# First loads as f32 by two other queues, f32 transposes, x in halves, and one written order, in a one-core attention and gated feed-forward kernel

## The chip, the core and the metric

The kernel runs on one core of a Trainium2 chip. The metric is the device time of one execution in microseconds, lower is better. A core has TensorE (PE, matmuls; its weight loads are listed as PEld), VectorE (DVE), ScalarE (ACT), GpSimd (POOL) and SyncE (SP). POOL, SP and ACT can issue DMAs, each from its own queue and in its own order; a DMA that changes the type of the data on the way is issued by POOL in this kernel.

## The reference, cut to what matters

```python
# attention: 4 batches, 8 heads, 768 positions, 64 per head, all f32
scores = q @ k.transpose(0, 1, 3, 2) / 8
# heads 0, 2, 6: causal; heads 1, 3, 4, 5, 7: the last 64 positions, and positions 0 to 3
a = softmax(where(mask, scores, -1e9))
x = (a @ v).transpose(0, 2, 1, 3).reshape(3072, 512)
# gated feed-forward on 3072 tokens
g = x @ w_gate                      # 512 x 1536
h = gelu(g) * (x @ w_val)           # 512 x 1536
ffn = h @ w_out                     # 1536 x 512
out = x + sigmoid(x @ w_res) * ffn  # 512 x 512
```

## The kernel before

The 3072 tokens are cut into six chunks of four 128-row tiles (`CHUNKS`; chunks 1 and 4 span two batches). For each chunk the kernel does attention for four pairs of heads (`PAIRS`: 0 = heads 0, 2; 1 = 4, 6; 2 = 1, 3; 3 = 5, 7), turns the result to features by tokens (`xT`), makes gate and value (`gate_value`; the blocks of the last six of twelve feature rows by a scheme with seven products for eight, `fast`, with copies `seed` and `hold` and sums `merge` between its matmuls), and then the output (`output`, `output_fast`, also with seven products: copies `keep`, sums `plus`).

Queries and keys are loaded by POOL, which makes f16 of them on the way, into `qks` (L678); for the first two chunks PE turns them (L824, `qkT`) and ACT or DVE evacuates (L835, `qkE`), later ones are turned by DMA (L868). Scores are L1012 (row tiling: two half-height matmuls side by side) and L1103 (first four keys, quarter tiling), exponentials L1028, L1032, L1110, masks L1064, weighted values L616 and L1136 (column tiling). A reciprocal (L1190) and a multiply (L1203, `norm`) give f32 `xtok`, and for chunk 0 and the odd heads a second multiply (L1201, `norm16`) gives f16 `x16`, which PE turns (L1225, evacuated by L1233, `xE`). `xtok` has two buffers of a whole chunk, [128, 4, 512] f32. Chunks 1 to 4 store x to the output (L1443, `store_x`), and the rest is added to it by DMA (L1522); chunks 0 and 5 add x on DVE or POOL (L1528, L1568) and store the sum (L1534, L1572).

Every operation is recorded as a task with the tasks that it needs and the buffers that it uses. `schedule` lays them out: a list per engine (`PLAN`, five lists of task numbers, and a sixth with buffer places) is followed by a model of the time, which also puts dummy matmuls (L1578, `warm`) where PE would stand. Each engine then runs its list in order and waits on semaphores. A PE task has a tiling (`mode`); tasks with `able` may also run in column tiling (matmuls of L617: two half-width ones), which is kept where the task before left it so:

```python
stay = tiling == t.mode or tiling in t.able
if not stay:
    tiling = next(iter(t.able), t.mode)
```

PSUM has eight banks. Each kind of use has its banks and a cap; the products of `fast` run in the three pairs that the first three gate and value blocks of the chunk used (`LANES`).

Of the kernel before, what the change touches and what calls it, by code (L numbers as in the profile page):

```python
# [4 lines left out]
NHEAD = 8  # L5
# [42 lines left out]
LANES = 3  # L48


HINTS = (
)

PLAN = (
# [83 lines left out]
class Task:  # L138
# [4 lines left out]
    def __init__(self, eng, dur, fn, deps, prio, bufs=(), fset=None, dma=0.0, order=(), name="", grp=None):  # L143
# [4 lines left out]
        self.users = []  # L148
        self.ready = 0.0
        self.end = None  # L150
        self.done = None
        self.signal = False
        self.name = name
        self.sem = None
# [24 lines left out]


class Pool:
    def __init__(self, items, caps=None):
        self.items = items
        self.caps = caps or {}
        self.held = {}
# [1494 lines left out]
```

## Time and profile before

| | |
|---|---|
| median of 3 runs (lowest, highest) | 264.08 us (262.93, 264.22) |
| profiled execution, span from first to last instruction | 261.9 us |
| TensorE clock granted, mean | 0.998 |
| PE, DVE, ACT, POOL busy | 253.3, 202.2, 169.0, 107.7 us |
| DMA packets, of these under 512 B | 102068, 88720 |
| HBM read, written | 29.36 MB, 10.49 MB |

The profile gives the span of the profiled execution; its own whole time isn't listed apart from the three runs, which lie 1.0 to 2.3 us above the span. Times in rows are microseconds from the start of the span. A group's row gives line, engine, operation, output<-inputs and shapes, then busy time, mean ns of one, and the idle time ahead with what ended it. PE matmuls are pipelined: the time between starts is the time that one takes up, and the listed duration is longer.

### The profile page before, as it was taken

The page shows a single profiled execution, that of the slowest core. Times are in us where ns is not written, and L with a number is a line of the kernel's source. Part 1 is how long each engine was busy: PE and PEld are TensorE (multiplying, and loading weights), DVE is VectorE, ACT ScalarE, POOL GpSimd, SP SyncE. Part 2 cuts the span into 40 slices and gives each one's busy share as a digit, 9 for nine tenths or more (in the row PEclk, how much of TensorE's full clock was granted, in tenths as well). Part 3 has the DMA queues.
Part 4 walks back from the last instruction along what each step waited for, and adds up shares of the span by engine and source line. Part 5 has one row for each costly group of instructions (what it writes and reads, how often), then busy time and mean ns, then how long its engine had stood idle before and what let it go on. Part 6 is the DMA issues. An engine that isn't in the chain of part 4 may idle for free.

```text
span 261.9 us, 8109 instructions
## 1 busy us (share of the span) xinstructions
PE 253.3 (97%) x3436; PEld 181.4 (69%) x3436; DVE 202.2 (77%) x443; ACT 169.0 (65%) x303; POOL 107.7 (41%) x146
## 2 busy tenths in 40 slices
PE   7899999999999999999999999999999998999992
PEld 5568655458577477667578577689687677788891
DVE  2587449788888987868988788978687986678974
ACT  2488537795676997467896566896465994564511
POOL 8899918970061964243998330001110040010032
PEclk9999999999999999999999999999999999999999
DMA  7999999999989999999999999607940029060003
GB/s 67 162 186 191 196 191 194 183 170 153 168 226 136 154 138 143 209 178 129 128 93 110 151 199 130 204 5 116 228 104 1 3 22 137 12 80 4 3 22 141
DMA packets 102068, 33.18 MB, mean 127 GB/s; under 512 B 88720, under 2 KB 97168, under 8 KB 102032
## 3 DMA queue, kind: packets, MB, share of 16 engines
q0 software_dynamic: 74704, 18.88, 82.4%
q1 hardware_dynamic: 27040, 13.52, 26.0%
q8 instruction: 27, 0.44, 0.8%
q10 hardware_dynamic: 288, 0.26, 0.3%
q14 instruction: 9, 0.07, 0.1%
HBM read 29.36 MB, written 10.49 MB: 152 GB/s over the span
## 4 chain that ended last, share of the span: by engine, by line
PE 93%; DMA 2%; DVE 1%; issue 1%; POOL 1%; DVEq 0%; POOLq 0%
PE ps L616 47%; PE ps L617 33%; PE ps L1012 6%; DMA qks<-in_q_dram 2%; PE ps L1136 2%; PE ps L1578 2%; PE ps L1225 2%; PE ps L824 1%; PE ps L1103 1%; POOL qks L678 1%; DVE otile L1518 0%; DVE otile L1528 0%; DVE xtok L1203 0%; DVE ea L1064 0%; DVE rcp L1190 0%
## 5 line engine op out<-in xcount | busy, mean ns | idle before, releaser
L1522 POOL DMA_DIRECT2D out_dram<-otile x16 | 14.9, 966 | 87.9 <-DVE otile L1518 65.8
L678 POOL DMA_DIRECT2D qks<-in_k_dram x37 | 31.4, 892 | 31.7 <-DMA kT<-qks 24.3
L616 PE MATMUL ps<-xT,wg 128*128 128x512 f16 (+1 forms) x172 | 38.7, 337 | 0.0
L1291 ACT ACTIVATE gact<-ps 128x512 f16<-128x512 f32 x38 | 21.9, 596 | 22.9 <-PE ps L616 14.8
L1293 DVE SCALAR_TENSOR_TENSOR hT<-gact,ps 128x512 f16<-128x512 f16 x38 | 25.9, 686 | 12.5 <-PE ps L616 6.7
L616 PE MATMUL ps<-xT,wv 128*128 128x512 f16 (+1 forms) x160 | 35.3, 334 | 0.0
L678 POOL DMA_DIRECT2D qks<-in_q_dram x37 | 31.0, 867 | 6.8 <-PE ps L824 6.8
L1365 DVE TENSOR_TENSOR ps<-ps,otile 128x256 f32<-128x256 f32 x60 | 25.0, 430 | 6.3 <-PE ps L617 2.6
L678 POOL DMA_DIRECT2D va<-in_v_dram x24 | 24.3, 1021 | 0.0
L1028 ACT ACTIVATE ea<-ps 128x1024 f16<-128x1024 f32 (+2 forms) x24 | 21.5, 917 | 3.9 <-PE ps L1012 3.7
L1383 ACT ACTIVATE gact<-ps 128x512 f16<-128x512 f32 x30 | 16.5, 594 | 10.4 <-PE ps L616 6.0
L616 PEld LDWEIGHTS ps<-xT,wg 128*128 128x128 f16 x172 | 16.6, 98 | 9.5 <-DVE hT L1293 0.4
L616 PEld LDWEIGHTS ps<-xT,wv 128*128 128x128 f16 x160 | 15.3, 98 | 10.6 <-issue 0.4
L1390 DVE SCALAR_TENSOR_TENSOR hT<-gact,ps 128x512 f16<-128x512 f16 x30 | 19.5, 682 | 3.3 <-PE ps L616 1.8
L617 PE MATMUL ps<-xT,wv 128*64 128x512 f16 (+1 forms) x168 | 20.8, 350 | 0.0
L616 PE MATMUL ps<-wo,hT 128*128 128x256 f16 (+1 forms) x114 | 18.8, 296 | 0.0
L1494 DVE TENSOR_TENSOR otile<-otile,ps 128x256 f32<-128x256 f32 x33 | 13.5, 418 | 6.7 <-PE ps L616 3.4
L1203 DVE TENSOR_TENSOR xtok<-ps,rcp 128x512 f32<-128x512 f32 (+1 forms) x28 | 17.1, 610 | 1.4 <-DVE rcp L1190 0.5
L1462 ACT ACTIVATE srs<-ps 128x512 f32<-128x512 f32 x22 | 13.2, 598 | 7.7 <-PE ps L617 6.5
L617 PE MATMUL ps<-xT,wg 128*64 128x512 f16 (+1 forms) x144 | 17.4, 344 | 0.0
L1012 PE MATMUL ps<-qT,kT 64*128 64x64 f16 (+4 forms) x391 | 16.6, 213 | 0.0
L1361 ACT ACTIVATE ps<-ps 128x256 f32<-128x256 f32 x25 | 9.2, 369 | 10.6 <-PE ps L617 6.9
(174 smaller groups left out, 597.8 us busy)
## 6 DMA issues: line engine op xcount, KB each, us to landing
out_dram<-xtok SPq DMA_DIRECT2D x4, 1024.0 KB, 5.3
out_dram<-otile POOLq DMA_DIRECT2D x16, 256.0 KB, 4.9
va<-in_v_dram POOLq DMA_DIRECT2D x24, 128.0 KB, 8.5
qks<-in_q_dram POOLq DMA_DIRECT2D x32, 64.0 KB, 5.2
qks<-in_k_dram POOLq DMA_DIRECT2D x32, 64.0 KB, 7.6
wv<-in_moe_w_val_dram POOLq DMA_DIRECT2D x3, 512.0 KB, 10.0
wg<-in_moe_w_gate_dram POOLq DMA_DIRECT2D x3, 512.0 KB, 8.1
wo<-in_moe_w_out_dram POOLq DMA_DIRECT2D x4, 384.0 KB, 19.6
```

The source lines that it names most:

```text
L616: return e.matmul(o, lhsT=lhsT, rhs=rhs, **k)
L617: return [e.matmul(o[h:h + 64], lhsT=lhsT[:, h:h + 64], rhs=rhs, **k) for h in (0, 64)][-1]
L678: return G.add(eng, issue, lambda e: e.dma_start(out_ap(), in_ap), deps, prio, bufs=bufs, dma=cost, name=name, grp=grp)
L1012: return [e.matmul(at(scr)[:, oo:oo + w], lhsT=side(BB, qb, low, 1)[half, k0:k0 + 128], rhs=side(BB, qb, low, 0)[half, qq:qq + w], start=T ...
L1028: return e.activation(out=o, in_=i_, func=AF.Exp, scale=SM_SCALE)
L1203: t2 = G.add("dve", c_dve(2 * n * 64), lambda e: e.tensor_tensor(out=xview(), in0=avv(0, DHEAD), in1=scale(), op=ALU.mult), [t1] + xdeps, ...
L1291: ta = G.add("act", c_act(512), (lambda gb=gb, ga=ga, gw=gw: lambda e: e.activation(out=at(ga)[:, :], in_=at(gb)[:, gw], func=AF.Gelu))(), ...
L1293: th = G.add("dve", c_dve(512), (lambda vb=vb, ga=ga, f=f, vw=vw: lambda e: e.scalar_tensor_tensor(out=hv(f), in0=at(ga)[:, :], scalar=0.5 ...
L1365: return G.add("dve", c_dve(256), lambda e: e.tensor_tensor(out=at(ps)[:, o], in0=at(ps)[:, BL], in1=at(es)[:, 0:256], op=ALU.add), deps, ...
L1383: ta = G.add("act", c_act(512), (lambda x=x, ga=ga, both=both: lambda e: e.activation(out=two(at(ga)[:, :]), in_=both(x), func=AF.Gelu))() ...
L1390: th = G.add("dve", c_dve(512), (lambda x=x, f=f, ga=ga, both=both: lambda e: e.scalar_tensor_tensor(out=two(hv(f)), in0=two(at(ga)[:, :]) ...
L1522: t = G.add("pool", 1.0, (lambda ot=ot, r0=r0: lambda e: e.dma_start(out[r0:r0 + 128, :], at(ot)[:, :], accum_op=ALU.add))(), ends + [stor ...
```

## The change

- Queries and keys of the first 256 rows are loaded as f32, without a change of type, by SP (five DMAs of 128 KB) and ACT (three). They go into the space of `hT`. PE turns them in f32, 128 columns (two heads) at a time, against an f32 identity; the evacuation makes f16 of them. Rows 256 to 511 still come through POOL.
- Attention output of chunk 0 is turned from f32 `xtok`; the second multiply `norm16` of chunk 0 is gone.
- `xtok` is three buffers of [128, 4, 256]: a chunk uses two, one for each half of the columns (heads 0 to 3, heads 4 to 7). `store_x` issues two DMAs, and adds of 512 columns become two of 256, except at the very end, where they were split already.
- `PLAN` is one list of all tasks with the engine for tasks that have a choice, and the number of dummies at each place (46 in all; 68 ran before); `PLACES` has the buffer places. No model of the time is left. Every use of PSUM may take any bank or pair (four pairs in place of three for the products of `fast`), and the constraints of order beside data are gone.
- DMAs of one queue that follow each other's landing share a semaphore.

```diff
+HALVED = 4
+PLAN = (
+    "0 1 214a 213s 16 215a 6 217s 218a 7 212s 8 4 216s 9 2 221 211 219s 15 3 17 220 222 10 11 223 w23 236 12 234 237d 224 "
+    "235d 225 w9 420 414 5 422 200 248 421 238 249a 201 244 239d 415 w1 242 246 423 243a w1 240 247d 261 245d 241a 227 228 "
+    "230a 424 251 w7 425 416 461 426 417 231d 428 229 418 226 427 431 432 433 434 202 430 435 419 w2 478 429 462 436 446 "
...
+    "1822 1803 1823 1825d 1826g 1828 1829 1827s 1830d 1831g 199 1832a "
 )
...
+        for x in "".join(PLAN).split():
+            if x[0] == "w":
+                for _ in range(int(x[1:])):
+                    t = next(fillers)
+                    t.bufs[0].fixed = t.bufs[0].pool.quiet("warm")
+                    if t.bufs[0].fixed is not None:
+                        place(t, "pe")
+            else:
+                t = self.tasks[int(x.rstrip("padgs"))]
+                place(t, {"p": "pe", "a": "act", "d": "dve", "g": "pool", "s": "sp"}[x[-1]] if x[-1] in "padgs" else t.eng)
...
-    P_x = Pool(many("xtok", 2, [128, 4, D_MODEL], FP32))
+    P_x = Pool(many("xtok", 3, [128, 4, 256], FP32))
...
-        "lane": (LANES, [(4, 5), (2, 3), (0, 1)]),
+    pairs, any_ = [(4, 5), (2, 3), (0, 1), (6, 7)], one(7, 6, 5, 4, 3, 2, 1, 0)
...
+                    if c == 0 and y == 0:
+                        for i in range(n):
+                            t = G.flex({on: (0.6, (lambda j=j, i=i, s_=gi, src=src: lambda e: e.dma_start(
+                                wide(rows(j, s_, i), 256).rearrange("p (h d) -> p h d", h=4),
+                                src[b, s_:NHEAD:2, lo + i * 128:lo + i * 128 + 128, :].rearrange("h p d -> p h d")))())
+                                for on in ("sp", "act")}, [], base + 4 * gi + 1 - j, bufs=[first], dma=0.5, name="hw", grp=f"hw{j}{gi}")
...
+                        if f32:
+                            return [e.transpose(out=at(scr)[:, (m * n + i) * 128:(m * n + i + 1) * 128],
+                                                in_=wide(rows(jj, p // 2, i) + p % 2 * 128, 128), identity=wide(2048, 128))
+                                    for m, (p, jj) in enumerate(items) for i in range(n)]
...
-        direct = c == 0 or heads[0] % 2
+        xb = xbuf[heads[0] // 4]
+        direct = c and heads[0] % 2
...
+        tp = G.add("pe", 2 * c_mm(128, n), lambda e: [e.transpose(
+            out=at(scr)[:, i * 128:(i + 1) * 128], in_=at(xbuf[cb // 2])[:, l0 + i, (cb % 2) * 128:(cb % 2) * 128 + 128], identity=wide())
+            for i in range(n)], xdeps + [t_wide], pr - 3, bufs=[xbuf[cb // 2], scr, early], name="xT32") if c == 0 else G.add("pe", c_mm(128, n), lambda e: [e.transpose(
...
-            laned = c > 0 and f < LANES
-            gb, ga = Buf(P_ps, "lane" if laned else kind), Buf(P_ga)
-            vb = gb if laned else Buf(P_ps, kind)
+            gb, ga = Buf(P_ps, kind), Buf(P_ga)
+            vb = Buf(P_ps, kind)
...
-            lane = lanes_[q % LANES]
-            ps, free = lane
+            ps = Buf(P_ps, "lane")
...
+        stored[c] = [G.add("sp", 0.65, (lambda y=y: lambda e: e.dma_start(
+            out[r0:r0 + 512, y * 256:y * 256 + 256].rearrange("(i p) d -> p i d", p=128), at(xbuf[y])[:, :, :]))(),
+            list(xtoks[y]), 1000 * c - 3500, bufs=[xbuf[y]], dma=1.3, name="xst") for y in (1, 0)]
...
-        xbuf, xtbuf, xtoks, xttoks = Buf(P_x), Buf(P_xt), {}, []
+        xbuf, xtbuf, xtoks, xttoks = [Buf(P_x), Buf(P_x)], Buf(P_xt), ([], []), []
```

Task numbers count the tasks in the order of their making; those that the prediction speaks of are, after the change: 212 to 219 the f32 loads, 220 and 221 POOL's keys and queries of rows 256 to 511, 234 to 241 the f32 transposes and their evacuations, 242 to 249 those of rows 256 to 511, 425 and 417 the first scores of heads 5, 7 and 1, 3, 465, 470 and 476 the last exponentials of chunk 0, 199 the dummy exponential, 735 and 734 chunk 1's stores of x.

More of the change, by code (lines that the diff above doesn't have):

```diff
@@ L181, with __init__, take, give @@
 class Pool:
-    def __init__(self, items, caps=None):
+    def __init__(self, items):
         self.items = items
-        self.caps = caps or {}
-        self.held = {}
-        self.free = [(0.0, i) for i in range(len(items))]
+        self.busy = set()
         self.last = [[] for _ in items]
-    def can(self, kind, t):
-        if kind in self.caps:
-            h = self.held.get(kind, [])
-            h[:] = [f for f in h if f is None or f > t]
-            if len(h) >= self.caps[kind]:
-                return False
-        return any(f <= t for f, _ in self.free)
-    def has(self, buf, t):
-        return self.can(buf.kind, t) and (buf.fixed is None or any(f <= t and i == buf.fixed for f, i in self.free))
-    def take(self, buf, t):
-        best = min(x for x in self.free if x[0] <= t and buf.fixed in (None, x[1]))
-        self.free.remove(best)
-        buf.slot = best[1]
-        buf.war = list(self.last[best[1]])
-        self.held.setdefault(buf.kind, []).append(None)
-    def give(self, buf, t):
-        h = self.held[buf.kind]
-        h.remove(None)
-        h.append(t)
-        self.free.append((t, buf.slot))
+    def take(self, buf):
+        assert buf.fixed not in self.busy
+        self.busy.add(buf.fixed)
+        buf.slot = buf.fixed
+        buf.war = list(self.last[buf.slot])
+    def give(self, buf):
+        self.busy.remove(buf.slot)
         self.last[buf.slot] = list(buf.users)
@@ L219, in __init__, with take, quiet, give @@
         self.at_, self.kinds = at_, kinds
-        self.free = {}
-        self.last = {}
-        self.held = {}
-        for cap, spots in kinds.values():
-            for sp in spots:
-                for b in sp:
-                    self.free[b] = 0.0
-                    self.last[b] = []
-    def spots(self, kind, t):
-        cap, spots = self.kinds[kind]
-        h = self.held.setdefault(kind, [])
-        h[:] = [f for f in h if f is None or f > t]
-        if len(h) >= cap:
-            return []
-        return [sp for sp in spots if all(self.free[b] <= t for b in sp)]
-    def can(self, kind, t):
-        return bool(self.spots(kind, t))
-    def has(self, buf, t):
-        sps = self.spots(buf.kind, t)
-        return bool(sps) and (buf.fixed is None or self.kinds[buf.kind][1][buf.fixed] in sps)
-    def take(self, buf, t):
-        sp = self.spots(buf.kind, t)[0] if buf.fixed is None else self.kinds[buf.kind][1][buf.fixed]
+        self.busy = set()
+        self.last = {b: [] for spots in kinds.values() for sp in spots for b in sp}
+    def take(self, buf):
+        spots = self.kinds[buf.kind]
+        sp = spots[buf.fixed]
+        assert not self.busy & set(sp)
+        self.busy |= set(sp)
         buf.slot = sp
-        for b in sp:
-            self.free[b] = 1e18
         buf.war = [u for b in sp for u in self.last[b]]
-        self.held[buf.kind].append(None)
-    def give(self, buf, t):
-        h = self.held[buf.kind]
-        h.remove(None)
-        h.append(t)
+    def quiet(self, kind):
+        spots = self.kinds[kind]
+        free = [(max([u.place for b in x for u in self.last[b] if u.eng != "pe"], default=-1), i)
+                for i, x in enumerate(spots) if not self.busy & set(x)]
+        return min(free)[1] if free else None
+    def give(self, buf):
+        self.busy -= set(buf.slot)
         for b in buf.slot:
-            self.free[b] = t
             self.last[b] = list(buf.users)
@@ L448, in schedule, with place @@
-        self.prog, self.order_, self.span = prog, order, max(free.values())
+        prog = {e: [] for e in ENGS}
+        order = []
+        places = [int(x) for x in "".join(PLACES).split()]
+        bufs = [b for b in dict.fromkeys(b for t in self.tasks for b in t.bufs) if b.kind != "warm"]
+        assert len(bufs) == len(places)
+        for b, x in zip(bufs, places):
+            b.fixed = x
+        tiling = None
+        fillers = iter([t for t in self.tasks if t.name == "warm"])
+        def place(t, e):
+            nonlocal tiling
+            assert all(d.pos is not None for d in t.deps), t.name
+            if t.alts:
+                t.eng, (t.dur, t.fn) = e, t.alts[e]
+            for b in t.bufs:
+                if b.slot is None:
+                    b.pool.take(b)
+                for u in b.war:
+                    if u is not t:
+                        t.deps.append(u)
+            if e == "pe":
+                if tiling != t.mode and tiling not in t.able:
+                    tiling = next(iter(t.able), t.mode)
+                t.run = tiling
+            t.pos, t.place = len(prog[e]), len(order)
+            prog[e].append(t)
+            order.append(t)
+            for b in t.bufs:
+                b.left -= 1
+                if b.left == 0:
+                    b.pool.give(b)
@@ L449, in schedule @@
+        assert len([t for t in order if t.name != "warm"]) == len([t for t in self.tasks if t.name != "warm"])
+        self.tasks = order
+        self.prog, self.order_, self.span = prog, order, 0.0
         return self.span
@@ L652, in build_kernel @@
     t_ident = G.add("pool", 0.3, aff(ident[:, :], ALU.not_equal, 1.0, 0, [[-1, 128]], 1), [t_ident], -58.5, name="const")
+    early = Buf(P_hs)
+    wide = lambda: at(early)[:, 0, 0, :, :].rearrange("p i k -> p (i k)").bitcast(FP32)
+    t_wide = G.add("dve", 0.2, lambda e: e.tensor_copy(out=wide(), in_=ident[:, :]), [t_ident], -52, bufs=[early], name="wide")
     t_causal = chain(-54, [(128, lambda e: e.memset(m_causal[:, :], 1.0)),
@@ L788, in loads_rows @@
         n = 2
+        first = Buf(P_h) if c == 0 else None
+        wide = lambda o, w: at(first)[:, :, :, :].rearrange("p f i k -> p (f i k)").bitcast(FP32)[:, o:o + w]
+        rows = lambda j, s_, i: ((j * 2 + s_) * 2 + i) * 256
+        if c == 0:
+            t_wide = G.add("dve", 0.2, lambda e: e.tensor_copy(out=wide(2048, 128), in_=ident[:, :]), [t_ident], -59, bufs=[first], name="wide")
         tok = {}
@@ L814, in loads_rows @@
             for k_ in range(0, NPAIR, per):
-                ps_ = sorted(ORDER[k_:k_ + per])
+                ps_ = list(range(k_, k_ + 2)) if c == 0 and y == 0 else sorted(ORDER[k_:k_ + per])
                 pr = 1000 * c - 492 + ps_[0] if c else 40 * k_ - 205 + 200 * y
@@ L1169, in weigh @@
             win = G.add("pe", 0.03 * n * len(near), windows(near, range(n)), deps, pr - 1,
-                           bufs=[P.et, av] + [u for b in both for u in (batch(b).v, batch(b).vs)], order=list(last), name=f"win{P.p}")
+                           bufs=[P.et, av] + [u for b in both for u in (batch(b).v, batch(b).vs)], name=f"win{P.p}")
             win.mode = "col"
@@ L1203, in weigh @@
         t2 = G.add("dve", c_dve(2 * n * 64), lambda e: e.tensor_tensor(
-            out=xview(), in0=avv(0, DHEAD), in1=scale(), op=ALU.mult), [t1] + xdeps, pr - 2 + (200 if c == 0 and heads[0] else 0), bufs=[av, rc, xbuf], name="norm")
-        for i in range(n):
-            xtoks.setdefault(l0 + i, []).append(t2)
-        if not direct:
+            out=xview(), in0=avv(0, DHEAD), in1=scale(), op=ALU.mult), [t1] + xdeps, pr - 2, bufs=[av, rc, xb], name="norm")
+        xtoks[heads[0] // 4].append(t2)
+        if c == 0:
+            xdeps.append(t2)
+        elif not direct:
             def cast(on):
@@ L1248, in gate_value @@
             pr = 1000 * c + 500 + f
-            if f < len(halves) * 2:
+            if halves and f < HALVED:
                 ths = []
```

295 lines of the change are left out of this document (64 added, 231 removed), and 154 rows, old and new, of tables (PLACES, PLAN).

## The prediction

> **What bounds the kernel now.** First the busy times and the chain that ended last:
>
> ```profile
> PE 253.3 (97%) x3436; PEld 181.4 (69%) x3436; DVE 202.2 (77%) x443; ACT 169.0 (65%) x303; POOL 107.7 (41%) x146
> PE 93%; DMA 2%; DVE 1%; issue 1%; POOL 1%; DVEq 0%; POOLq 0%
> ```
>
> TensorE is on the chain for 93% of the span. A busy PE can hide waits, so I cut the span where the kind of work changes (window view: length, then busy us and count of PE, its weight loads, DVE, ACT, POOL; granted clock; DMA share; GB/s), and took the dummy matmuls of L1578 by themselves (second fence), then the waits of PE.
>
> ```profile
> 0.00:1.13 1.13, 0.00 (x0) 0.00 (x1) 0.22 (x2) 0.32 (x1) 0.20 (x4) 1.00 0.00 0
> 1.13:6.28 5.15, 5.15 (x29) 3.69 (x29) 1.20 (x5) 1.17 (x2) 4.93 (x6) 1.00 0.80 77
> 6.28:10.33 4.05, 2.87 (x48) 1.78 (x47) 1.39 (x3) 1.19 (x2) 3.93 (x9) 1.00 1.66 157
> 10.33:20.87 10.54, 10.53 (x184) 7.10 (x184) 9.00 (x26) 8.78 (x19) 9.63 (x18) 1.00 1.67 178
> 20.87:27.35 6.48, 6.48 (x118) 5.49 (x116) 5.13 (x18) 5.25 (x9) 6.48 (x9) 1.00 1.38 200
> 27.35:257.13 229.78, 228.30 (x3064) 163.35 (x3061) 183.43 (x389) 152.32 (x272) 81.57 (x104) 1.00 1.08 123
> 257.13:261.94 4.81, 0.00 (x0) 0.00 (x0) 1.86 (x3) 0.00 (x0) 0.99 (x1) 0.89 0.37 136
> ```
> ```profile
> 0.00:27.35 27.35, 11.81 (x68) 6.73 (x68) 1.00 1.37 154
> ```
> ```profile
> PE ps L1136 <- issue: 1.2, 1, 1.2
> ```
>
> The reader is to see three stretches. From 27.35, where the first chunk's attention output has been turned, to the last matmul at 257.13, PE is idle for 229.78 - 228.30 = 1.48 us, 1.2 of it in one place (in the last chunk's attention). Ahead of that, 68 dummies fill 11.8 us, and 1.1 + 1.2 us are empty: there PE waits for data. Behind it are 4.8 us without PE. So only four things can move the time: the work PE has, the waits in the front, the 1.48 us, and the tail. One part of PE's work isn't matmul, its changes of tiling:
>
> ```profile
> 43.25 0.38 PE L616 MATMUL ps<-xT,wg 128*128 128x512 f16 x1
> 43.46 1.03 PE L616 MATMUL ps<-xT,wv 128*128 128x512 f16 x4
> 44.42 0.45 PE L1103 MATMUL ps<-qT,kT 64*32 64x256 f16 x16
> ```
>
> Each 512-column matmul starts 43.46 - 43.25 = 0.21 us after the one before. Four from 43.46 are streamed by 44.32, and the next, of the quarter tiling, starts at 44.42: 0.1 us for the change.
>
> **The change, part by part.**
>
> *Front.* These rows set it (chain of waits, then timeline, then the time to landing of the first loads):
>
> ```profile
> 3.22 5.73 DMA qks<-in_q_dram
> ```
> ```profile
> 1.35 1.88 POOL L678 DMA_DIRECT2D qks<-in_k_dram  x2 [0.84 <-POOLq L1662]
> 10.34 0.46 PE L1012 MATMUL ps<-qT,kT 64*128 64x128 f16 x14
> 10.37 0.80 POOL L636 TENSOR_SCALAR_AFFINE_SELECT m_win<-m_win 128x256 f16<-128x256 f16 x2
> 15.55 0.42 DVE L1201 TENSOR_TENSOR x<-ps,rcp 128x256 f16<-128x256 f32 x1
> 20.44 0.59 ACT L1028 ACTIVATE es<-ps 128x512 f16<-128x512 f32 x1
> ```
> ```profile
> DMA to landing us min/median/max: 4.4/5.7/6.5
> out_dram<-otile ACTq DMA_DIRECT2D x2, 128.0 KB, 1.8
> out_dram<-otile SPq DMA_DIRECT2D x2, 128.0 KB, 2.4
> ```
>
> Before, POOL issues all six loads of the first 512 queries and keys, the first queries land at 3.22 + 5.73 = 8.95, and the first scores run at 10.34. After, eight loads of 128 KB leave SP (five) and ACT (three) from about 1, when PE starts too. Stores of that size land after 1.8 to 2.4 us, but these move 256-byte pieces, eight at a time, so I take 4.5 for the first queries, 6 for the keys. The new order puts 23 dummies ahead of the first transposes (29 before, 5.15 us: 23 take 4.1, to 5.2), and the first scores come at about 7.5, 2.8 us earlier.
>
> But rows 256 to 511 stay on POOL. The new order has POOL make six small constants (0.40 each for the larger, some 2 us) ahead of its first DMA, so this goes out at about 2.9 in place of 1.35, and the two land at 2.9 + 4.8 = 7.7 and about 3.8 + 5.7 = 9.5. PE's order has their transposes ahead of those of heads 1, 3, 5 and 7 of the first rows, with seven dummies behind: scores of these heads at about 11.8. From there I walked the order: PE's own work to the next-to-last scores (17.4), then ACT's last three exponentials, 0.59 to 1.02 each, end at about 19.5. Before, the last one ended at 20.44 + 0.59 = 21.03. Gain 1.5 us, not 2.8. Behind it PE is dense in both kernels, so what is left of the gain is 1.5 less the dearer transposes behind that point (next). Bounds: nothing, if the loads land later, to 2.9, if nothing waits at all: filler and empty time are 1.1 + 5.15 + 39 x 0.11 + 1.2 = 11.8 before and, by the new order, 1.1 + 4.1 + 23 x 0.11 = 7.7 after, and 1.2 of the 4.1 between goes to dearer transposes.
>
> *Transposes in f32.* Sixteen for the first queries and keys (there were 32 of half width), sixteen for the first chunk's attention output. Rows of the f16 ones and of dummies (chain of waits):
>
> ```profile
> 9.84 0.35 PE ps L824 x8
> 15.00 0.44 PE ps L1578 x4
> 62.38 0.22 PE ps L1225 x4
> ```
>
> A 128-wide f16 transpose takes 0.22 / 4 = 0.055 us. No f32 matmul is in the trace. Bounds: 0.055 (the same columns) and four times that, 0.22; I take 0.11, by the bytes. Queries and keys: 16 x 0.11 = 1.8 against 4 x 0.35 = 1.4; output: 16 x 0.055 = 0.9 more, half of it behind the exponentials above. Net of the front: 1.5 - 0.45, I take 1.1 gained.
>
> The Trainium skill, "FP8 and Floating Point Precision", section "TensorE Precision Notes", has true FP32 at four passes through the array; the trace shows no f32 and so neither agrees nor disagrees. By it the sum below would lose its sign (first rival); by 0.11 it stands.
>
> *Removed second scaling (norm16 of chunk 0).* Eight DVE operations of L1201, 0.42 each (the row at 15.55 above), 3.4 us; DVE has room there (9.00 of 10.54), and the transposes wait for the same reciprocal and one multiply as before. Zero.
>
> *One global order.* I read both orders against the tiling each task asks for. Behind the last transposes of chunk 0 PE changes tiling 74 times before and 61 times after: 13 x 0.1, 1.3 us gained. As PE is dense there, nothing hides it. The order also hands DVE more of what ACT did: nine `seed`, six `hold`, eight `keep`, and three each of the evacuations of transposes (`qkE`, `xE`), these spread out:
>
> ```profile
> L1361 ACT ACTIVATE ps<-ps 128x256 f32<-128x256 f32 x25 | 9.2, 369 | 10.6 <-PE ps L617 6.9
> L1362 DVE COPY ps<-ps 128x256 f32<-128x256 f32 x5 | 2.2, 431 | 0.3 <-PE ps L616 0.2
> 67.00:85.00 18.00, 18.00 (x128) 12.31 (x126) 15.38 (x33) 11.54 (x27) 4.93 (x7) 1.00 1.23 182
> ```
>
> 23 x 0.43 = 9.9 us over five chunks, 2 each: 15.4 + 2 of 18 in such a stretch. Bounds 0 to 9.9; it still fits, and the paired banks of a product have four places in place of three, so I take 0. The 1.48 us of waits I leave as they are (0 to some 3 after).
>
> *x in column halves.* Six more DVE adds (a 512 split in two), twice 0.42 for 0.69 (rows of the tail, below), 0.9 us in all on an engine with room: zero. Four more stores on SP. Three half buffers in place of two whole ones: while chunk 0 holds two for its output, chunk 1 has one. Its second half (heads 4 to 7) can be written only when its first half's store has landed.
>
> ```profile
> out_dram<-xtok SPq DMA_DIRECT2D x4, 1024.0 KB, 5.3
> ```
>
> The store waits in SP's queue behind a transposing load, and 5 us more is its landing; some 4 us of PE and DVE work lie between the two writes in the order. DVE then stands for 1 to 2 us, with the chunk-0 sums queued behind it; PE has 2.2 us of gate and output work queued ahead of the next transposes, of which 1.5 are used by the chain itself. Bounds 0 to 2; I take 0.4 lost.
>
> *Tail.* (timeline, then chain of waits)
>
> ```profile
> 254.85 0.73 POOL L1528 TENSOR_TENSOR otile<-otile,xtok 128x256 f32<-128x256 f32 x1 [0.36 <-DVE otile L1518]
> 256.27 0.85 PE L617 MATMUL ps<-wt,hT 128*64 128x256 f16 x12
> 257.22 0.42 DVE L1518 SCALAR_TENSOR_TENSOR otile<-srs,ps 128x256 f32<-128x256 f32 x1 [0.23 <-PE ps L617]
> 257.56 0.83 DVE L1518 SCALAR_TENSOR_TENSOR otile<-srs,otile 128x256 f32<-128x256 f32 x1
> 258.43 0.69 DVE L1528 TENSOR_TENSOR otile<-otile,xtok 128x512 f32<-128x512 f32 x1
> ```
>
> Before, DVE is done at 258.43 + 0.69 = 259.12, 2.0 us after PE. After, the second residual product comes one task before the end, so the last two gated operations (0.42 each) follow PE by up to 0.9, and the last add is split: DVE 0.42, POOL 0.73. 0.9 + 0.73 + 0.1 = 1.7: 0.3 gained, between 0.6 and a loss of 0.3. The dummy exponential that loaded ACT's table at the start now stands ahead of ACT's last store; the load lies beside those 1.7 us.
>
> **Sum.** -1.1 - 1.3 + 0.4 - 0.3 = -2.3. The profiled span of 261.94 becomes 259.7. The median of the runs, 264.08, lies 2.1 above that span, for what is around it; kept, it gives 261.8.
>
> **The rivals.**
> First, slower: an f32 transpose takes 0.22. 32 x 0.11 = 3.5 more, nearly all on PE's path: 265.3. It decides from 0.18 each (2.3 / 32 more than 0.11); from 0.22, with any further wait, it is slower. For it: twice the bytes and no row. Against: a transpose only moves numbers.
> Second, the third half buffer holds chunk 1 up for 2.6 us, as when the store lands after 6 us and more: 264.0. For it: DMA is crowded there; against: work queued on PE.
> Third, the early loads are hidden anyway: the scores of rows 256 to 511 still wait for POOL, the front gains nothing, 262.9. For it: POOL starts 1.5 us later.
> Fourth, better: nothing waits in the front (1.8 more) and the order also ends the 1.48 us of waits: 258.5 to 260. For it: both are waits on order, not on a resource.
> Fifth, DVE becomes the bound: a third of the 9.9 us falls on PE: 265.1. For it: 17.4 of 18; against: it still fits.
>
> **How the numbers follow.** Forecast 0.50, own range 260.3 to 263.3; rivals in order 0.15, 0.06, 0.08, 0.15, 0.06. Half a per cent, 1.3 us, is about what a measurement of this kernel can tell from no change. Faster: 0.85 of the forecast and the fourth, 0.58. Same: the rest of the forecast, second, third, 0.22. Slower: first and fifth, 0.20. The range, 258.0 to 266.0: down to all of the fourth, up to the first with the store's wait.
>
> **What would show it.** Right: first scores at about 7.5, last exponential of chunk 0 near 19.5, f32 transposes at 0.11 from start to start, 61 changes of tiling at 0.1, PE idle 1 to 3 us from there to the end, DVE near 213 us. Wrong: f32 rows at 0.2 or more, a DVE wait for the `xtok` store at 60 to 65 us, or new PE waits for DVE in the later chunks.

## The result and the profile after

The changed kernel takes 261.57 us (median of 5 runs, 260.82 to 261.93), the one before 263.23 (5 runs beside it, 262.93 to 264.22): a ratio of 0.9923 with a 95% interval of 0.9899 to 0.9947. A second set of runs gave 0.9932 (0.9902 to 0.9962). The forecast was 261.8. The profiled span went from 261.9 to 259.6 us. These 2.3 us are those of one pair of executions; by the medians the gain is 1.7 us in the first set of runs and 2.5 in the second (263.91 to 261.38).

The page's busy times and chain, and the window view cut where the work changes (first dummy, first transposes, first scores, end of chunk 0's last exponential, end of its last transposes, last matmul, end):

```profile
PE 250.9 (97%) x3378; PEld 181.9 (70%) x3378; DVE 208.1 (80%) x473; ACT 155.2 (60%) x273; POOL 105.8 (41%) x143
PE 83%; DVE 5%; DMA 5%; ACT 2%; issue 1%; POOL 1%; POOLq 0%; DVEq 0%
```
```profile
1.13:6.01 4.88, 4.88 (x23) 3.43 (x24) 1.73 (x6) 1.28 (x1) 4.54 (x9) 1.00 0.95 184
6.01:8.43 2.42, 2.42 (x20) 2.08 (x19) 1.51 (x3) 0.00 (x0) 2.37 (x4) 1.00 1.70 192
8.43:18.75 10.32, 9.80 (x192) 7.13 (x191) 7.89 (x24) 9.24 (x20) 9.37 (x15) 1.00 1.74 185
18.75:23.16 4.41, 4.41 (x70) 4.03 (x68) 3.38 (x13) 3.48 (x9) 1.86 (x3) 1.00 1.55 195
23.16:254.35 231.19, 229.37 (x3084) 165.25 (x3081) 191.81 (x425) 139.75 (x244) 85.64 (x108) 1.00 1.01 125
254.35:259.64 5.29, 0.00 (x0) 0.00 (x0) 1.61 (x3) 1.48 (x2) 1.54 (x2) 0.98 0.31 115
```

The reader is to see that the front is shorter by far more than the span: chunk 0's last transposes end at 23.16, not 27.35. Of these 4.2 us, 1.9 are, by a count of the matmuls on both sides, work that now comes later (two half-width gate and value pieces of 0.43 us each and two groups of f16 transposes of 0.5): a gain of 2.3. The last exponential says the same: it ended at 21.03 and ends at 18.15 + 0.60 = 18.75. From there the dense part takes 231.19 us against 229.78; less the 1.9 that moved into it, it is 0.5 shorter. The tail is 5.29 against 4.81. So 2.3 + 0.5 - 0.5 = 2.3, the span's difference.

The rows behind it (chain of waits; timeline; waits of PE; timeline of DVE; timeline of the end):

```profile
2.92 6.07 DMA qks<-in_q_dram
11.37 0.45 PE ps L710 x4
22.73 0.44 PE ps L1100 x4
```
```profile
8.43 0.51 PE L884 MATMUL ps<-qT,kT 64*128 64x128 f16 x13
16.37 0.56 PE L884 MATMUL ps<-qT,kT 64*128 64x256 f16 x11
18.15 0.60 ACT L900 ACTIVATE es<-ps 128x512 f16<-128x512 f32 x1
```
```profile
PE ps L1008 <- issue: 1.4, 1, 1.4
```
```profile
63.17 0.69 DVE L1076 TENSOR_TENSOR xtok<-ps,rcp 128x512 f32<-128x512 f32 x1 [0.32 <-DMA out_dram<-xtok]
```
```profile
253.49 0.86 PE L488 MATMUL ps<-wt,hT 128*64 128x256 f16 x12
253.97 0.96 POOL L1393 TENSOR_TENSOR otile<-otile,xtok 128x256 f32<-128x256 f32 x1 [0.95 <-DVE otile L1383]
254.36 0.85 DVE L1383 SCALAR_TENSOR_TENSOR otile<-srs,otile 128x256 f32<-128x256 f32 x1
255.13 0.41 DVE L1383 SCALAR_TENSOR_TENSOR otile<-srs,ps 128x256 f32<-128x256 f32 x1
255.58 0.42 DVE L1393 TENSOR_TENSOR otile<-otile,xtok 128x256 f32<-128x256 f32 x1
255.62 0.96 POOL L1393 TENSOR_TENSOR otile<-otile,xtok 128x256 f32<-128x256 f32 x1 [0.69 <-DVE otile L1383]
256.67 0.36 ACTq L1399 DMA_DIRECT2D out_dram<-otile  x1
```

The f32 transposes (L710 for queries and keys, L1100 for the output) start 0.11 us apart. The wait of L1008 that the chain puts down to "issue" is 1.4 us in the last chunk, where the kernel before had 1.2 at L1136. DVE waits 0.32 us for the store of chunk 1's first half. In the end the gated operation between two SBUF tiles takes 0.85 us, twice as long as that on PSUM, while POOL, which began first, adds beside it. At 255.58 DVE begins first: its add keeps 0.42, and the POOL add beside it, which the store waits for, takes 0.96.

### The profile page after: what moved, and what is told of

Same layout as the page of the kernel before. It is cut to its first block, busy times and chain, and to the rows that moved or that the text cites. A ratio compares the mean times of both kernels' runs of the same rounds, so it can differ in the third digit from the quotient of the medians.

```text
span 259.6 us, 8008 instructions
## 1 busy us (share of the span) xinstructions
PE 250.9 (97%) x3378; PEld 181.9 (70%) x3378; DVE 208.1 (80%) x473; ACT 155.2 (60%) x273; POOL 105.8 (41%) x143
## 4 chain that ended last, share of the span: by engine, by line
PE 83%; DVE 5%; DMA 5%; ACT 2%; issue 1%; POOL 1%; POOLq 0%; DVEq 0%
PE ps L487 42%; PE ps L488 31%; PE ps L884 5%; DMA qks<-in_q_dram 2%; PE ps L1008 1%; DMA out_dram<-otile 1%; PE ps L713 1%; DMA out_dram<-xtok 1%; DVE xtok L1076 1%; PE ps L1102 1%; PE ps L1100 1%; PE ps L975 1%; DVE otile L1383 1%; DVE otile L1429 0%; POOL m_win L505 0%
## 5 line engine op out<-in xcount | busy, mean ns | idle before, releaser
L550 POOL DMA_DIRECT2D qks<-in_q_dram x35 | 32.1, 981 | 30.8 <-DMA kT<-qks 13.5
L487 PE MATMUL ps<-xT,wv 128*128 128x512 f16 (+1 forms) x172 | 38.9, 337 | 0.0
L550 POOL DMA_DIRECT2D va<-in_v_dram x24 | 24.9, 1041 | 18.3 <-PE ps L1008 10.5
L487 PEld LDWEIGHTS ps<-xT,wv 128*128 128x128 f16 x172 | 16.7, 98 | 11.8 <-DVE hT L1260 0.4
L1260 DVE SCALAR_TENSOR_TENSOR hT<-gact,ps 128x512 f16<-128x512 f16 x30 | 19.5, 681 | 2.0 <-PE ps L487 1.1
L488 PE MATMUL ps<-xT,wv 128*64 128x512 f16 (+1 forms) x144 | 18.3, 344 | 0.0
L884 PE MATMUL ps<-qT,kT 64*128 64x64 f16 (+3 forms) x391 | 15.4, 213 | 0.0
L488 PE MATMUL ps<-wo,hT 128*64 128x256 f16 x216 | 15.3, 274 | 0.0
```

The lines of the kernel that those rows point to most:

```text
L487: return e.matmul(o, lhsT=lhsT, rhs=rhs, **k)
L488: return [e.matmul(o[h:h + 64], lhsT=lhsT[:, h:h + 64], rhs=rhs, **k) for h in (0, 64)][-1]
L550: return G.add(eng, issue, lambda e: e.dma_start(out_ap(), in_ap), deps, prio, bufs=bufs, dma=cost, name=name, grp=grp)
L884: return [e.matmul(at(scr)[:, oo:oo + w], lhsT=side(BB, qb, low, 1)[half, k0:k0 + 128], rhs=side(BB, qb, low, 0)[half, qq:qq + w], start=T ...
L1260: th = G.add("dve", c_dve(512), (lambda x=x, f=f, ga=ga, both=both: lambda e: e.scalar_tensor_tensor(out=two(hv(f)), in0=two(at(ga)[:, :]) ...
```

## The experiments

All are edits of the changed kernel; "after" is that kernel as it stands. Spans are of one profiled execution each; the runs of after have spans of 258.7 to 260.5 us, and between its two profiles, 259.6 and 260.2, 0.4 of the 0.6 us is the one wait at "issue", which is 1.2 to 2.1 us in the ten profiles here that have it. From here on its size is the time from the start of the matmul ahead of it to the start of the one behind; the views of waits give some 0.2 less.

**The front undone.** In place of the eight f32 loads, four by POOL as f16, turned in f16.

```diff
-  t = G.flex({on: (0.6, ... dma_start(wide(rows(j, s_, i), 256) ...)) for on in ("sp", "act")}, ...)
+  t = dma("pool", base, 0.7, ... src[b, gi:NHEAD:2, lo:lo + 256, :].rearrange("h (p j) d -> p h (j d)", j=n), bufs=[st[j]])
-  f32 = c == 0 and y == 0
+  f32 = False
```

> The changed kernel with its front undone: the first 256 rows of queries and keys are loaded by POOL as f16 again (four DMAs at the head of its queue) and turned in f16, half width; all else as after. Theory (the front gave some 2.3 us, 21.03 to 18.75 at chunk 0's last exponential): first scores near 10.3 in place of 8.43, the last exponential at 20.5 to 21.5, span 261.3 to 262.3 in place of 259.6. Rival (early loads are hidden, the gain is the rest of the order): last exponential within 0.5 of 18.75, span 259.3 to 260.1.

Measured: ratio to before 1.0109 (1.0071 to 1.0148), span 265.2, first scores 12.33, and the last exponential ends at 24.46, 5.7 us late. That is more than the theory said. The waits of PE put it down to the edit's own order, POOL's six loads and its masks in each other's way (timeline of ACT, then waits of PE):

```profile
23.86 0.60 ACT L906 ACTIVATE es<-ps 128x512 f16<-128x512 f32 x1
```
```profile
PE ps L890 <- DVE kT L733: 3.7, 1, 3.7
PE ps L719 <- POOL ident L505: 1.5, 1, 1.5
```

So a second version had the identity and the first two loads at the head of POOL's queue, then the masks, then the other loads.

```diff
-  212 213 217 216 214 215 2 4 218 219 6 7 8 9 10 11
+  2 212 213 6 7 8 4 9 10 11 217 216 214 215 218 219
```

> As e1_undo_loads (first 256 rows by POOL as f16), but POOL's order is changed: f16's identity, the two loads of heads 0, 2, 4, 6, then all constants of the masks, then the other loads. In e1_undo_loads the first loads had landed at 4.73 and 5.56 and PE waited for the identity to 6.90 and for DVE behind a mask to 12.33. Theory (SP's and ACT's queues give the front its 2.3 us): scores of the first heads may come at 8.5 to 9.5, but every later load leaves POOL some 2 us or more later than after, and the last exponential comes at 20 or later, span 261 to 263. Rival (the order of POOL's queue alone gives it): last exponential by 19.3, span 259.2 to 260.2.

Measured: 1.0098 (1.0077 to 1.0118), span 263.7. The timeline of PE and ACT:

```profile
8.59 0.51 PE L890 MATMUL ps<-qT,kT 64*128 64x128 f16 x13
10.43 0.41 PE L719 MATMUL ps<-ident,qks 128*64 128x128 f16 x8 [1.34 <-DMA qks<-in_q_dram]
12.72 0.64 PE L719 MATMUL ps<-ident,qks 128*64 128x128 f16 x16 [1.87 <-DMA qks<-in_k_dram]
22.57 0.60 ACT L906 ACTIVATE es<-ps 128x512 f16<-128x512 f32 x1
```

First scores come as early as after's (8.43), so it isn't the first load that the other queues win. It is all that follows it in POOL's queue: PE waits 3.2 us for later loads, and the last exponential ends at 23.17, 4.4 us late. The theory holds, though the span is past its 261 to 263, and the order of POOL's queue isn't enough; but the rest of the order was made for the other loads, so 4.4 us isn't the price of the queues alone. 1.4 us of this span belong to another wait, at 70 us, told below.

**POOL's own loads earlier.** The loads of rows 256 to 511 ahead of POOL's constants.

```diff
-    "0 1 214a 213s 16 215a 6 217s 218a 7 212s 8 4 216s 9 2 221 211 219s 15 3 17 220 222 ..."
+    "0 1 2 221 220 214a 213s 16 215a 6 217s 218a 7 212s 8 4 216s 9 211 219s 15 3 17 222 ..."
```

> The changed kernel with the two POOL loads of rows 256 to 511 (and f16's identity, ahead of them) moved ahead of the five small constants of POOL, so that the first leaves at about 1.1 us in place of 2.92. Theory (these loads set the front: they stand in the chain of waits): they land 1.5 us earlier, the last exponential of chunk 0 comes 0.7 to 1.5 us before 18.75, span 258.1 to 259.0. Rival (PE's and ACT's own work sets the front by now, or the earlier loads delay the f32 ones beside them): last exponential within 0.3 us, span 259.3 to 260.

Measured: 0.9969 (0.9945 to 0.9993), span 260.7, last exponential 18.93. The theory fell. Of the rival the last exponential came as it said, but not the span, 259.3 to 260. The queries' load left POOL at 1.92 us, one us earlier, and landed at 8.98, as in after (8.99); the keys' landed at 10.41 against 10.24. PE turned them no sooner (timeline, then the chain of waits):

```profile
9.21 0.41 PE L713 MATMUL ps<-ident,qks 128*64 128x128 f16 x8
```
```profile
7.29 0.23 DVE m_win L516
8.12 0.61 DVE kT L724
8.77 0.51 PE ps L884 x11
```

In after these loads stand in the chain of waits, but here an earlier issue didn't make them land earlier. What landed later was a neighbour: the f32 load that SP issues at 3.0 us took 5.8 us, against 4.7 to 5.0 in the ten other profiles with this front, both of after among them. So the loads seem to share what the DMAs can give by then (184 to 192 GB/s in the window rows above); that wasn't tried by itself. And the edit has a price of its own: the constants now come behind the loads, so a copy of a mask on DVE starts only at 7.29, its evacuations and the first scores (8.77) follow, and PE turns the queries behind those, 0.18 us later than in after (9.03). The last exponential is late by the same 0.18. The loss of 1.1 us is a wait of 1.1 us at 57.5, for a copy `vs` that landed at 58.5 and not at 56.0.

**f16 for the output of chunk 0.** The second multiply is back, into a tile of its own; PE turns the f16 copy.

```diff
+            xdeps.append(G.add("dve", ..., out=x16c[:, cb0:cb0 + 2, l0:l0 + n, half], in0=avv(0, DHEAD), in1=scale(), ...))
-            out=at(scr)[...], in_=at(xbuf[cb // 2])[...], identity=wide())
+            out=at16(scr)[...], in_=x16c[:, cb, l0 + i, :], identity=ident[:, :])
```

> The changed kernel with f16 back for chunk 0's attention output: eight more DVE operations (0.42 each, 3.4 us) ahead of the multiplies to xtok write an f16 copy, and PE turns that, 16 transposes at 0.055 in place of 0.11. Theory (PE is the bound, DVE has room): PE does 0.9 us less, half of it ahead of the last exponential, span 258.9 to 259.6. Rival (DVE's 3.4 us stand on the path to the transposes in the front, since a DVE order holds them up): last transposes of chunk 0 later than 23.16, span 260 to 261.

Measured: 0.999 (0.9964 to 1.0016), span 263.2. The rival held: PE does less, and yet the front ends later. ACT's last exponential and the waits of PE (us in total, times, longest):

```profile
19.21 0.60 ACT L902 ACTIVATE es<-ps 128x512 f16<-128x512 f32 x1 [0.73 <-PE ps L886]
```
```profile
PE ps L886 <- DVE xtok L1078: 0.6, 2, 0.3
PE ps L1105 <- DVE xtok L1078: 0.4, 1, 0.4
```

Scores (L886) wait for a bank that DVE has yet to read: 18.75 becomes 19.81, and the last transposes end at 24.32 in place of 23.16. In this order the second multiply costs 1.1 us, net of the dearer transposes. The other 2.4 us of the span come behind it, among them 1.3 us at 87 us, where PE starts right behind a transposing load of queries (landed at 87.11, in after at 84.26), and 0.5 more at the wait of the last chunk. The profiled execution took 265.01 us, and the median of the 12 is 262.91: by the medians the kernel loses 1.3 to 1.5 us, little more than the front's 1.1.

**Four half buffers of x.**

```diff
-    P_x = Pool(many("xtok", 3, [128, 4, 256], FP32))
+    P_x = Pool(many("xtok", 4, [128, 4, 256], FP32))
```

> The changed kernel with four half buffers of xtok in place of three, so that chunk 1's second half has its own. Theory (the store's wait costs nothing, as work lies queued): DVE's wait of 0.32 us at 63.17 is gone, PE's last matmul and the span stay within 0.3 us of 254.35 and 259.6. Rival (it still costs the 0.4 us predicted or more): span 259.2 or less, and the gain begins at 60 to 65 us.

Measured: 0.9924 (0.9895 to 0.9954), span 259.4, PE's last matmul at 254.10. DVE's wait is gone and nothing is gained, as the theory said. But the wait isn't harmless: in the kernel with eight dummies more (below) the same store landed 5.3 us after its issue, not 3.3, and then (timeline of DVE, waits of PE)

```profile
66.38 0.69 DVE L1076 TENSOR_TENSOR xtok<-ps,rcp 128x512 f32<-128x512 f32 x1 [2.32 <-DMA out_dram<-xtok]
```
```profile
PE ps L487 <- DVE otile L1359: 1.8, 1, 1.8
```

PE stood 1.8 us behind it; so it did 1.4 us in both versions of the undone front, at 70 to 72 us.

**More changes of tiling.** Every output product of chunks 3 and 4 takes the other tiling than the task before it.

```diff
+                if t.name == "fw" and t.able and 5300 <= t.prio < 7000:
+                    tiling = None if tiling == "col" else "col"
                 t.run = tiling
```

> The changed kernel in which the output products of chunks 3 and 4 switch between untiled and column tiling at every task: 114 changes of tiling behind chunk 0's last transposes in place of 61, the same order and the same columns. Theory (0.1 us for a change, nothing hides it): 53 x 0.1 = 5.3 us more, span 264.9. Rival (a change costs nothing by itself; the 0.1 us in the rows is that of small matmuls after it): span within 0.5 us of 259.6. Between them lies a hidden part: 1 to 4 us.

Measured: 1.0094 (1.0062 to 1.0125), span 263.6, PE's last matmul at 258.35. The same stretch by windows:

```profile
23.16:258.35 235.19, 234.85 (x2967) 158.91 (x2965) 192.52 (x425) 140.24 (x243) 85.75 (x108) 1.00 1.00 123
```

PE's busy time here rises from 229.37 to 234.85: 5.48 us for 53 changes, 0.103 each, as the theory had it. The span rises less, since the wait at "issue" isn't there in this kernel (0.34 us idle in place of 1.82).

**Another end.** The gated operation on PSUM first, each add behind its own half, both on DVE, two stores of half a tile.

```diff
-    "... 1828 1829 1827s 1830d 1831g 199 1832a "
+    "... 1829 1831d 1827s 1869s 1828 1830d 199 1832a "
```

> The changed kernel with another end: the last tile's two gated operations in the other order (that on PSUM first), each add behind its own half only, both adds on DVE and none on POOL, and two stores of 128 KB in place of one of 256 KB. Theory (the end is the chain of DVE and POOL behind PE's last matmul, 0.85 us of it an operation made twice as long by a POOL add beside it, 0.96 a POOL add): gated on PSUM ends near 255.0, the last add near 256.3, span 0.35 to 0.6 shorter, 259.0 to 259.3, if PE ends at 254.35. Rival (the last store's landing sets the end, and two stores land no earlier): span within 0.2 of 259.6.

Measured: 0.9899 (0.9872 to 0.9926), median 260.89. PE ends at 254.58 and the span at 258.75: 4.17 us behind PE in place of 5.29.

```profile
254.69 0.42 DVE L1384 SCALAR_TENSOR_TENSOR otile<-srs,ps 128x256 f32<-128x256 f32 x1
255.15 0.42 DVE L1395 TENSOR_TENSOR otile<-otile,xtok 128x256 f32<-128x256 f32 x1
255.49 0.42 DVE L1384 SCALAR_TENSOR_TENSOR otile<-srs,otile 128x256 f32<-128x256 f32 x1
255.94 0.42 DVE L1395 TENSOR_TENSOR otile<-otile,xtok 128x256 f32<-128x256 f32 x1
256.40 0.36 ACTq L1401 DMA_DIRECT2D out_dram<-otile  x1
```

All four run at 0.42 now; with no POOL add beside it the gated operation on SBUF is back from 0.85. The last store is issued 1.8 us behind PE in place of 2.3 and lands in 1.8 in place of 2.0; what is left of the 1.1 lies behind the landing (0.6 us in place of 0.9). That is about twice what the theory gave. By the runs alone the gain isn't sure, as the intervals of the two kernels overlap.

**The wait at "issue".** In after it lies between the first and the second matmul of one task, where no semaphore is. Counting PE's instructions in the trace, matmuls, weight loads and semaphore events, it falls on number 5825 in before and 5569 in after: 256 apart, and both 193 modulo 256. The trace also has a queue that carries instructions (packets, MB, share):

```profile
q8 instruction: 26, 0.43, 0.7%
```

These 26 packets are 16 KB each, one for some 263 of PE's 6829 records. The trace also dates them. In all ten profiles with the wait, PE starts again 1.2 to 1.4 us after the last such packet has landed (in after at 215.98, the packet at 214.63), while the wait itself runs from 1.2 to 2.1; at no boundary in the fourteen does a block start sooner behind its packet than 1.2. That packet left 1.9 to 3.2 us after PE had begun the block of 256 before (in after at 213.68, the block at 211.46), and this block is used up in 3.0 to 3.9. In the four profiles without the wait, the packet left within 0.7 us of the block's start. By these dates PE stands for its next instructions, and what decides is when their packet leaves.

To move the boundary, eight dummies of 16 columns were added in the front, 16 instructions:

```diff
+    [e.matmul(at(warm)[:, 0:m_], ...) for m_ in [256] + ([16] * 8 if w_ == 32 else [])]
```

> The changed kernel with eight dummy matmuls of 16 columns more in the front, where PE waits for an evacuation (16 instructions of PE with the weight loads, less than 0.1 us on the path). PE's wait of 1.5 us in the last chunk, inside a run of small matmuls without a semaphore, fell on recorded instruction 193 of 256 in before, after and e2_four_halves. Theory (PE's instructions come in blocks of 256 by DMA, and this block is used up in 3.0 us, faster than the next one comes): the wait moves back by 16 instructions, to recorded number 193 modulo 256 again, and as the block ahead of it then takes 3.7 us, it is 0.8 us or less, span 258.7 to 259.2. Rival (it is a wait at this matmul for data): the wait stays at the same matmul with 1.3 to 1.8 us.

Measured: 1.0019 (0.9995 to 1.0043), span 263.0, slower than after. The wait moved back by 16 instructions into another task and stands at number 5569 again, so the theory holds on its place; on its size it failed, for it is 1.9 us and not 0.8: the block ahead takes 3.7 us, but the packet left 3.2 us after it had begun. The profiled execution took 266.24 us, and the median of the 12 is 263.96. The rest of the loss is the store of x (above) and the copy `vs`, both landing later.

**The moves back to ACT.** All 38 `seed`, `hold` and `keep` copies that DVE makes go to ACT.

```diff
-    "... 1808d 1806 1794 1842a 1807 1843 1797 1810 1809d ..."
+    "... 1808a 1806 1794 1842a 1807 1843 1797 1810 1809a ..."
```

> The changed kernel with all 38 copies seed, hold and keep that the order gives to DVE made by ACT (14, 10 and 14; 16 us of DVE's work). Theory (DVE had room, so where the copies run costs nothing): DVE near 192 us, ACT near 170 us, span within 0.7 us of 259.6, no new PE wait over 0.5 us for DVE or ACT. Rival (DVE's load of 80% has become part of the bound): span 258.6 or less. Third (ACT, whose exponentials and gelus the matmuls wait for, holds them up now): span 260.5 or more.

Measured: 1.0011 (0.999 to 1.0032), span 262.4, with after at 0.9932 beside it. The third case: PE's largest waits for another engine are now for ACT,

```profile
PE ps L487 <- ACT otile L1354: 1.2, 2, 0.7
PE ps L488 <- ACT otile L1354: 0.5, 1, 0.5
```

and DVE, at 195.2 us in place of 208.1, gives nothing back. The kernel is then no faster than the one before, though the edit moves more than the change did: of such copies the kernel before had 15 on DVE. And the order was made with them on DVE, so this doesn't price the 23 that the change moved.

**Together.** The end and the four halves, then the same with 16 of the first dummies cut into two of 128 columns; after ran beside them.

```diff
+    [e.matmul(at(warm)[:, 0:m_], ...) for m_ in ([128, 128] if w_ < 16 else [256])]
```

> The changed kernel unchanged, as the measure for the three beside it. All theories: ratio to before between 0.990 and 0.995, span 259 to 260; the wait of PE in the last chunk at recorded instruction 193 of 256 again, 1.3 to 2.1 us.

> The changed kernel with the end of e6_tail and the four half buffers of e2_four_halves. Theory (the end gives 1.1 us, 4.17 in place of 5.25 behind PE's last matmul; the fourth buffer gives nothing where the store lands in 3.3 us and takes away a wait of DVE of up to 2.3 us where it lands later): span 258.2 to 258.9, ratio to before 0.986 to 0.990. Rival (the earlier end of e6_tail was chance): span 259.2 or more.

> As c1_tail_halves, with 16 of the first dummies of 256 columns cut into two of 128: the same columns in the front, 32 instructions of PE more with the weight loads. Theory (the wait in the last chunk belongs to the boundary of a block of 256 instructions, and is gone where the boundary falls as in e1_undo_loads, whose PE had 31 recorded instructions more and no wait): no wait over 0.5 us at 210 to 222, span 1.3 to 2 us under c1_tail_halves. Rival (how late the next block comes is chance, not the place): 1.3 to 2.1 us at recorded number 193 modulo 256, span as c1_tail_halves.

Measured: after 261.38 us, 0.9932 (0.9902 to 0.9962), span 260.2, the wait 2.0 us at number 5569. Tail and halves: 260.08, 0.9891 (0.9852 to 0.993), span 257.7 (forecast 258.2 to 258.9), the wait 1.2 us. With 32 instructions more: 258.96, 0.9832 (0.9802 to 0.9862), the fastest kernel here, 2.4 us under after. The waits of PE in the last two, in this order:

```profile
PE ps L1012 <- issue: 1.0, 1, 1.0
```
```profile
PE ps L491 <- DVE ps L1241: 0.7, 2, 0.3
PE ps L491 <- ACT es L904: 0.3, 1, 0.3
```

In the second no wait at "issue" is left, as the theory said; but its span is only 0.2 us shorter, not 1.3 to 2, since PE waits 0.8 us more at 152 us; why there was not tried. By the medians it is 1.1 us faster; the profiled execution of tail and halves took 259.42 us, 0.7 under its median.

## Why the prediction was right, and where only its sum was

The total was predicted at -2.3 us of span and came out at -2.3, in one pair of profiles. Its terms didn't, so the total is in good part luck. So is the nearness of 261.57 to 261.8: the forecast counted from 264.08, the median of three runs before, and five runs gave 263.23, from which -2.3 makes 260.9.

| step | predicted | measured |
|---|---|---|
| front, with the f32 transposes | -1.1 | -2.3 |
| 13 changes of tiling fewer | -1.3 | -1.3 (13 x 0.103, by the slope) |
| store of the x half | +0.4 | 0 here, 1.4 to 1.8 in three variants |
| all else in the dense part | 0 | +0.8 (what the 0.5 leaves of the 1.3) |
| tail | -0.3 | +0.5 |

*Front.* Two steps failed and make up the 1.2 us. The walk ended the last exponential at 19.5, and it ended at 18.75. And the dearer transposes were to lose 0.45 behind it, but from there to the last transposes it took 6.3 us before and 4.4 + 1.9 = 6.3 after, so nothing was lost. The prediction counted changes of tiling only behind the front; in the front the trace has 44 before and 24 after, 8 and 3 of them in this last stretch, where five fewer at 0.103 would be the missing 0.5. The dates on the way were forecast too early (first scores 7.5, measured 8.43 and 7.9 to 8.5 in other kernels with this front; the two POOL loads 7.7 and 9.5, measured 8.99 and 10.24), and the walk after them too long: next-to-last scores at 17.4, measured from 16.37. These two errors cancelled in part; where the walk was too long isn't shown.

"Removed second scaling ... Zero", argued from DVE's 9.00 busy of 10.54, was wrong as well. An average of 85% hides that, of the operations queued behind a multiply, one frees the bank of the next scores; with the multiply back the front lost 1.1 us. But this isn't a term to add to the predicted 1.1, as the walk followed the new order, in which the multiply is already gone. How the front's 2.3 divides among loads, multiply and changes of tiling stays open: 4.4 and 1.1 are prices in an order made for the change, and they don't add up to it.

The 11.8 us that 68 dummies were said to fill are listed durations, which overlap with other matmuls; by the time between starts it is 5.15 + 39 x 0.11 = 9.4, as the prediction's own bound has it.

*Transposes in f32.* 0.11 was right, so the first rival never came. The Trainium skill, "FP8 and Floating Point Precision", section "TensorE Precision Notes", has true FP32 at four passes; here a transpose of 128 columns takes 0.11 us in f32 against 0.055 in f16, twice and not four times, and the measurement decides.

*Tiling.* The price of 0.1 and "nothing hides it" held where it was tried, in the output products of chunks 3 and 4, and the counts of 74 and 61 are those of the traces.

*x in halves.* The mechanism was right, the second rival's too, and DVE's wait at 63.17, a sign of being wrong by the prediction's list, did come, but PE didn't wait behind it. Which of them it is hangs on one landing: 3.3 us costs PE nothing, 4.9 costs 1.4 and 5.3 costs 1.8 (the prediction had 0.4 at a landing of 5 and 2.6 at 6 and more).

*Waits.* Of the 0.8 us, 0.3 are idle time of PE, 1.82 against 1.48 in the window rows; the rest is what the sum leaves, short waits inside PE's busy time by the look of the one that was followed, 0.39 us at 73.75 for a `hold` of ACT whose tile was still being stored. Whatever the copies moved to DVE brought or cost is in it too. The 1.2 us in the last chunk was "left as is" rightly, but the fourth rival called it a wait on order. It belongs to the block of 256 instructions that begins there. The Trainium skill, "Runtime: NRT & Kernel Launch", section "Instruction fetch mechanics", states blocks of 256 instructions that a queue of the sequencer's own fetches ahead, with a cost mostly hidden; the trace agrees on the block (256 between the two kernels, a move by 16 with 16 more), and on a hidden cost at nearly all other boundaries, but this one cost 1.2 to 2.1 us in ten profiles and nothing in four. Why the packet leaves late in the ten stays open. The time in which the block ahead is used up doesn't decide it, 3.0 us in after and 3.7 in the kernel with eight dummies, both with the wait, but 3.2 in the last kernel, without it. The place may: the kernels with 31 or 32 recorded instructions more than after, three of the four without the wait, all lack it, and those with as many as after or up to 16 more all have it.

*Tail.* The sum of 0.9 + 0.73 + 0.1 left out that a POOL add that has begun first doubles a DVE operation between two SBUF tiles (0.85 for 0.42), and that a POOL add which begins behind one takes 0.96, not 0.73. A row for the first stood in the prediction's own quote, the 0.83 at 257.56, beside this one (timeline of the kernel before):

```profile
256.74 1.38 POOL L1528 TENSOR_TENSOR otile<-otile,xtok 128x512 f32<-128x512 f32 x1 [1.15 <-DVE otile L1518]
```

The Trainium skill, "SBUF — State Buffer", section "Who interferes with whom", gives DVE and GpSimd one shared pair of ports, held by one at a time; the rows agree, since the operation that reads PSUM stayed at 0.42 (at 257.22) beside that POOL add, which ran from 256.74 to 258.12.

*DVE as the bound.* Nothing here speaks for the fifth rival: behind the front PE's only wait for DVE that the waits view lists in after is 0.2 us, and taking 13 us from DVE made the kernel slower, with PE's new waits for ACT. The 213 us forecast for DVE left out the 3.4 of the removed multiplies; 209.6 would have been near the 208.1 measured.

## What to carry over

A busy share of 85% doesn't make work on that engine free: ask which operation queued behind it frees a bank or releases a transfer, and price that one. Where several transfers share the DMAs, issuing one earlier need not make it land earlier, and a wait that costs nothing at a landing of 3 us can cost 2 at a landing of 5, so a buffer more is insurance that a single profile doesn't price. A total that comes out right is no proof of its terms: the front and the tail here were each off by about a microsecond, in opposite directions.

## What was not expected of the hardware

PE's instruction stream can stall: 1.2 to 2.1 us at a boundary of 256 instructions, with no semaphore near, until 1.2 to 1.4 us after a packet of instructions has landed. An f32 transpose of 128 columns costs twice an f16 one (0.11 us for 0.055). And small edits far away shift landings: the copy `vs` landed near 58.5 in two kernels and at 56.0 in after, the store of x took 5.3 us in one and 3.3 in after, and whole spans moved by 1 to 3 us.
